# Rearranging the opening of a tuned Fourier-mixing and GEGLU kernel, and starting its first chunk's second layer sooner

## The chip, the cores and the metric

The kernel runs on one core of a Trainium2 chip. The metric is the device time of one execution in microseconds (us); lower is better. The profile's span (first to last instruction) is about 2 us shorter than the device time (632.1 and 633.91 us in the profiled run of the kernel before). Engines are named as in the profile: PE is TensorE (PEld its weight loads), DVE is VectorE, ACT is ScalarE, POOL is GpSimd, and SPq is the queue of DMA issues of SyncE. L695 is line 695 of the kernel that the profile belongs to, so the same statement has another number after the change.

## The reference

```python
# x: (8, 3008, 256); w_gate, w_val: (256, 1536); w_out: (1536, 256); all float32
X = np.fft.fft(x, axis=1)
X = np.fft.fft(X, axis=2)
y = X.real.reshape(24064, 256)
g = y @ w_gate
gelu = 0.5 * g * (1.0 + erf(g / sqrt(2)))
out = (gelu * (y @ w_val)) @ w_out
```

## The kernel before

Each of the 8 batches is folded (rows t and -t are added), transformed by matmuls into `EO`, and sent through the two layers in three chunks of 512 or 481 columns. A chunk has 12 *slots*, one for each 128 of the 1536 hidden features; there are 288 slots. A slot has five layer-1 matmuls on PE, two GELUs on ACT, three vector operations on DVE and one product on POOL. The layer-2 work of a chunk is 24 pieces of four matmuls, done two to a slot in the slots of the *next* chunk; the transform of the next batch fills gaps ("fill"), and POOL folds the batch after. Before slot 0 stands the opening: it builds the transform's constants, loads and folds batch 0, and makes the first weights.

The opening, with fillers (`warm`, dummy matmuls that keep PE busy):

```python
    def opening():
        # x of rows 9 to 16 and 0 loaded plainly by SyncE, then POOL's queue:
        pool_consts()
        pool_consts2()                      # holds the 1.35 us iota into par
        index_consts(0)
        cast_mirror(0, 9, 8)                # first gather of x
        cast_forward(0, 1, 8)
        cast_mirror(0, 5, 4)
        cast_mirror(0, 1, 4)
        index_consts(1)
        cast_mirror(0, 0, 1)
        for f0, n in ((0, 256), (256, 256), (512, 1024)):
            load_w(f0, n)
        for q in range(4):
            load_wo(q)
        # ...
        warm(11)
        vec_consts()
        g_phases()
        # ... more constants on DVE and ACT
        t_columns()
        t_phases()
        t_sin()
        warm(10)
        # ... gelu_table, t_write, identities, cw_rest, then:
        fold_piece(9, 4)
        stage1(2)
        warm(4)
        fold_piece(13, 4)
        fold_piece(5, 4)
        warm(2)
        stage1(1)
        warm(3)
        fold_piece(0, 1)
        stage1(3)
        warm(2)
        fold_piece(3, 2)
        fold_piece(1, 2)
        stage1(0)
        make_w(0, 0, 256, engine="V")()
        ch(0, 0)()
        ch(0, 1, "V")()
        make_w(1, 0, 256, engine="V")()
        tp_e(0, 0)()
        tp_o(0, 0, "V")()
```

The loads of batch 2 and the loop over the slots. `load_part` issues a plain load from SyncE and a gather from POOL (the mirrored rows):

```python
        for k, s in ((0, 18), (1, 19), (2, 19)):
            at(fill, s, lambda k=k: load_part(2, k))
        # ...
        for i, (parts, fc) in enumerate(blocks):
            if fc == 0 and i:
                assert not pend
                pend = list(works[i // NFC - 1])
            parts["G"][fc]()
            if i == 0:
                behind_first_gate()
            if before:
                before[0]["g"][before[1]]()
            parts["V"][fc]()
            if pend:
                pend.pop(0)()
            for f in pool.pop(i, []):
                f()
            if before:
                before[0]["v"][before[1]]()
            if pend:
                pend.pop(0)()
            for f in fill.pop(i, []):
                f()
            before = parts, fc
```

SyncE issues one after another: stores of a finished group of 128 tokens, and in every batch from the third on the write of the half-transformed batch to memory and its read in another layout (`z_read`):

```python
    def z_read(b):
        def run():
            st = state(b)
            st["Z"] = Z_tile()
            z = z_dram[b % 2]
            n = (NK // 2) * C
            nc.sync.dma_start(
                out=_sub(st["Z"], [[1, n]], 0), in_=ap_replace(z, ap=[[n, 128], [1, n]], offset=z.offset))
        return run
```

## Time and profile before

| before | us |
|---|---|
| median of the first 3 runs | 634.19 (633.90 to 634.34) |
| span of the profiled run | 632.1 |
| first layer-1 matmul (gate, E half; then O half) | 20.47; 21.11 |
| first GELU of slot 0, 12, 17, 25, 31, 287 | 21.52, 45.86, 59.22, 77.01, 91.32, 614.95 |

The slot times are starts of the first GELU of a slot (L638 in the timeline).

PE is nearly always busy (98%), so I looked for time where it is not: in the opening, in the first chunk and at stalls.

The chain of waits of the kernel before in the opening (start, length, what):

```profile
1.54 1.35 POOL par L281
3.42 0.56 POOL idx L268
...
4.26 5.73 DMA xb<-in_x_dram,idx
...
11.79 1.46 PE ps_o L757 x4
...
17.09 0.56 DVE A_sb L475
...
20.36 0.71 DVE EO_sb L556
```

A POOL fill, an index column and the gather's 5.73 us come first; then fillers (L757) at half clock (the clock record reads 0.50 from 11.9 us on for 3.4 us) stand in front of stage 1.

The timeline of the kernel before, with the first folds of batch 2 and the layer-2 matmul that waited behind them (the bracket is the idle time of the engine before the instruction, and what ended it):

```profile
20.47 0.38 PE L622 MATMUL ps_g<-EO_sb,W_sb 128*128 128x512 bf16 x1
21.11 0.38 PE L622 MATMUL ps_g<-EO_sb,W_sb 128*128 128x512 bf16 x1 [0.26 <-DVE EO_sb L556]
...
75.97 0.21 POOL L216 TENSOR_TENSOR ab_sb<-x_raw,x_raw 94x8 f32<-94x8 f32 x1 [1.80 <-DVE ve_sb L656]
...
80.92 0.28 PE L695 MATMUL ps_o<-Wo_sb,h_sb 128*128 128x256 bf16 x1 [0.32 <-POOL h_sb L671]
```

The windows view of the kernel before (busy time of PE, PEld, DVE, ACT, POOL; then the clock granted to TensorE, 1.00 being full speed, DMA share, GB/s):

```profile
80.00:85.00 5.00, 4.68 (x36) 2.90 (x34) 3.66 (x7) 3.60 (x9) 5.00 (x5) 1.00 0.32 81
```

### The profile page before, as it was taken

To read this page: it belongs to the slowest core of one execution; us is meant where nothing else is said; L and a number is where in the kernel's file an instruction comes from. 1 tells how busy PE (TensorE), PEld (TensorE's weight loads), DVE (VectorE), ACT (ScalarE), POOL (GpSimd) and SP (SyncE) were. 2 spreads that over 40 slices of the span, in tenths; PEclk is the share of its full clock that TensorE was granted. 3 is DMA by queue.
4 is the path that set the end of the run, shared out by engine and by line. 5 is a ranking of instruction groups with operands and counts; after the bars stand their busy time and mean duration, and the time that the engine had idled before them with its cause. 6 is when DMAs were issued, how large, how long until landed. Compare 5 with 4: busy or idle time off the path is not lost.

```text
span 632.1 us, 13032 instructions
## 1 busy us (share of the span) xinstructions
PE 618.9 (98%) x4285; PEld 407.4 (64%) x4285; DVE 580.9 (92%) x937; ACT 432.7 (68%) x855; POOL 505.7 (80%) x511
## 2 busy tenths in 40 slices
PE   7999999999999999999999999999999999999997
PEld 3446666666666666666666666666666666666666
DVE  7698889999899989999999999999999999999992
ACT  6787777666766667666776767766776766666651
POOL 8599799989997998879998799968988555555651
PEclk8999999999999999999999999999999999999999
DMA  8931925535454352633635325633222232221123
GB/s 152 179 61 26 250 63 147 139 99 138 121 146 107 91 140 65 167 84 100 156 93 155 93 66 138 153 92 104 57 53 57 75 104 54 52 51 38 43 51 80
DMA packets 51994, 63.84 MB, mean 101 GB/s; under 512 B 7783, under 2 KB 47194, under 8 KB 49530
## 3 DMA queue, kind: packets, MB, share of 16 engines
q1 hardware_dynamic: 45238, 47.23, 28.9%
q0 software_dynamic: 6096, 15.29, 11.5%
q8 instruction: 33, 0.54, 0.3%
q10 hardware_dynamic: 592, 0.49, 0.3%
q14 instruction: 35, 0.29, 0.1%
HBM read 38.86 MB, written 29.38 MB: 108 GB/s over the span
## 4 chain that ended last, share of the span: by engine, by line
PE 87%; DMA 4%; DVE 3%; POOL 2%; ACT 2%; issue 1%; POOLq 0%; DVEq 0%; ACTq 0%
PE ps_o L695 36%; PE ps_g L622 27%; PE ps_v L622 17%; DMA Z_sb<-z 3%; PE ps_dft L508 2%; PE ps_dft L544 2%; POOL h_sb L671 1%; DVE v_sb L669 1%; DMA xb<-in_x_dram,idx 1%; DVE h_sb L667 1%; PE ps_o L757 1%; PE ps_dft L574 1%; ACT gelu_sb L638 1%; DVE ve_sb L656 1%; PE ps_g L695 0%
## 5 line engine op out<-in xcount | busy, mean ns | idle before, releaser
L671 POOL TENSOR_TENSOR h_sb<-gelu_sb,v_sb 128x512 bf16<-128x512 bf16 (+1 forms) x288 | 328.7, 1144 | 106.3 <-DVE v_sb L669 92.0
L695 PE MATMUL ps_o<-Wo_sb,h_sb 128*128 128x256 bf16 (+1 forms) x2232 | 334.9, 273 | 1.0 <-POOL h_sb L671 1.0
L695 PEld LDWEIGHTS <-h_sb 128*128 128x128 bf16 (+1 forms) x2304 | 228.8, 100 | 112.5 <-POOL h_sb L671 2.7
L656 DVE SCALAR_TENSOR_TENSOR ve_sb<-EB_sb,yw,ps_v 128x512 f32<-128x512 bf16 (+1 forms) x288 | 212.1, 737 | 32.8 <-PE ps_v L622 29.0
L638 ACT ACTIVATE gelu_sb<-ps_g 128x512 bf16<-128x512 f32 (+1 forms) x288 | 169.6, 589 | 96.4 <-PE ps_g L622 93.0
L622 PE MATMUL ps_g<-EO_sb,W_sb 128*128 128x512 bf16 (+1 forms) x864 | 231.2, 375 | 2.7 <-ACT gelu_sb L647 2.0
L622 PE MATMUL ps_v<-EO_sb,W_sb 128*128 128x512 bf16 (+1 forms) x576 | 214.4, 375 | 0.5 <-ACT W_sb L423 0.5
L667 DVE TENSOR_TENSOR h_sb<-gelu_sb,ps_v 128x512 bf16<-128x512 bf16 (+1 forms) x288 | 195.0, 677 | 1.1 <-ACT gelu_sb L647 0.7
L669 DVE SCALAR_TENSOR_TENSOR v_sb<-ve_sb,ps_v 128x512 f32<-128x512 f32 (+1 forms) x288 | 192.6, 669 | 0.0
L622 PEld LDWEIGHTS <-W_sb 128*128 128x128 bf16 x1440 | 136.8, 98 | 82.3 <-issue 4.2
L647 ACT ACTIVATE gelu_sb<-ps_g 128x512 bf16<-128x512 f32 (+1 forms) x288 | 169.1, 587 | 0.0
L714 ACT ACTIVATE out_sb<-ps_o 128x512 f32<-128x512 f32 x92 | 54.9, 597 | 36.1 <-PE ps_o L695 36.0
L224 POOL TENSOR_TENSOR eo_sb<-ab_sb 94x512 bf16<-94x512 f32 (+1 forms) x60 | 66.6, 1110 | 0.1
L554 ACT ACTIVATE EO_sb<-ps_dft 128x512 bf16<-128x512 f32 (+1 forms) x44 | 26.0, 590 | 22.5 <-PE ps_dft L544 20.5
L511 ACT ACTIVATE S_sb<-ps_dft 96x512 bf16<-96x512 f32 x48 | 28.2, 587 | 11.3 <-PE ps_dft L508 11.3
L217 POOL TENSOR_TENSOR ab_sb<-x_raw,x_raw 94x508 f32<-94x508 f32 (+1 forms) x30 | 33.0, 1101 | 0.0
L220 POOL TENSOR_TENSOR ab_sb<-x_raw,x_raw 94x508 f32<-94x508 f32 (+1 forms) x30 | 32.9, 1096 | 0.0
L158 POOL DMA_INDIRECT x_raw<-in_x_dram,idx x18 | 17.0, 945 | 2.8 <-issue 0.6
L508 PE MATMUL ps_dft<-eo_sb,G 94*96 94x256 bf16 x102 | 19.2, 274 | 0.0
L544 PE MATMUL ps_dft<-TP,Z_sb 128*128 128x128 bf16 (+1 forms) x188 | 18.2, 218 | 0.5 <-DVE Z_sb L496 0.5
L544 PEld LDWEIGHTS <-Z_sb 128*128 128x128 bf16 x192 | 14.5, 98 | 2.4 <-DVE Z_sb L496 0.7
L757 PE MATMUL ps_o<-gelu_sb 128*128 128x512 bf16 x32 | 11.1, 498 | 1.2 <-DVE col L305 1.2
(128 smaller groups left out, 173.5 us busy)
## 6 DMA issues: line engine op xcount, KB each, us to landing
out_dram<-out_sb SPq DMA_DIRECT2D x361, 64.0 KB
x_raw<-in_x_dram SPq DMA_DIRECT2D x10, 768.0 KB
Z_sb<-z SPq DMA_DIRECT2D x6, 768.0 KB
z<-S_sb SPq DMA_DIRECT2D x6, 576.0 KB
EB_sb<-yrow SPq DMA_DIRECT2D x14, 128.0 KB
x_raw<-in_x_dram SPq DMA_DIRECT2D x2, 640.0 KB
z<-S_sb SPq DMA_DIRECT2D x6, 192.0 KB
EB_sb<-yrow SPq DMA_DIRECT2D x7, 120.2 KB
```

The costliest lines, as they stand in the source:

```text
L217: eng.tensor_tensor(ab(0, 1, up), fwd(1, up), mir(255, down), op=ALU.add)
L224: eng.tensor_tensor(_sub(eo, [[C, nj], [1, 128]], j0 * C + g * 128), ab(0, 0, [[1, 128]]), ab(1, 0, [[1, 128]]), op=op)
L544: nc.tensor.matmul(ps[:, o : o + n], st["Z"][:, pair, g * 128 : g * 128 + 128], _sub(TP, [[1, n]], g * 128), start=True, stop=True)
L622: nc.tensor.matmul(ps[:, :n], W[nm, part][:, fs], src, start=start, stop=stop, **kw)
L638: nc.scalar.activation(gl[:, 0, :n], pg[:, :n], AF.Gelu)
L647: nc.scalar.activation(_sub(gl, [[-1, n]], TOK + n - 1), pg[:, :n], AF.Gelu)
L656: nc.vector.scalar_tensor_tensor(ve[:, :n], EB_bufs[b][:, c0 : c0 + n], yw[:, fc : fc + 1], pv[:, :n], op0=ALU.mult, op1=ALU.add)
L667: nc.vector.tensor_tensor(st["h"][:, fc, 0, :n], gl[:, 0, :n], pv[:, :n], op=ALU.mult)
L669: nc.vector.scalar_tensor_tensor(_sub(vv, [[-1, n]], n - 1), ve[:, :n], 2.0, pv[:, :n], op0=ALU.mult, op1=ALU.subtract)
L671: nc.gpsimd.tensor_tensor(st["h"][:, fc, 1, :n], gl[:, 1, :n], vv[:, :n], op=ALU.mult)
L695: nc.tensor.matmul(pso[:m, half], st["h"][:, fc, sign, h0 : h0 + m], Wo_sb[:, fc, :], start=(fc == 0), stop=(fc == NFC - 1),)
L714: nc.scalar.activation(_sub(osb, [[1, 2 * C]], 0, part_num=m), pso[:m, :], AF.Copy)
```

## The change

The intent: issue the gather of x before the constants; compute fewer phases, and share the rest between engines; place fewer fillers (12 + 3 + 6 instead of 11 + 10 + 4 + 2 + 3 + 2); issue the second batch's x casts in one run ahead of slot 0; put POOL's folds of batch 1 out of slots 11 to 13; and do six of the first chunk's layer-2 pieces in slots 6 to 14.

```diff
@@ index: written as integers, no float column
-        nc.gpsimd.iota(col_i[:, i : i + 1], pattern=[[0, 1]], base=base, channel_multiplier=-1, **IOTA)
+        nc.gpsimd.memset(idx, 0)
+        nc.gpsimd.iota(idx[:NP, :], pattern=[[0, 1]], base=base, channel_multiplier=-1)
@@ opening, POOL's queue
         pool_consts()
-        pool_consts2()
         index_consts(0)
         cast_mirror(0, 9, 8)
+        pool_consts2()
+        cast_mirror(0, 5, 4)
         cast_forward(0, 1, 8)
-        cast_mirror(0, 5, 4)
-        cast_mirror(0, 1, 4)
         index_consts(1)
         cast_mirror(0, 0, 1)
-        for f0, n in ((0, 256), (256, 256), (512, 1024)):
+        cast_mirror(0, 1, 4)
+        for f0, n in ((0, 256), (256, 256), (512, 512), (1024, 512)):
             load_w(f0, n)
... (w_out in two loads instead of four)
+        xb[1] = xb_tile(1)
+        cast_forward(1, 9, 8)
+        cast_mirror(1, 9, 8)
+        cast_forward(1, 0, 9)
+        for j0, nj in ((5, 4), (1, 4), (0, 1)):
+            cast_mirror(1, j0, nj)
@@ opening, the rest (identities, CW and TP writes move from ACT to DVE,
@@ phases from DVE to ACT; helpers cut)
-        warm(11)
+        warm(12)
... (constants)
-        warm(10)
... 
+        warm(3)
+        fold_piece(9, 4)
+        t_reduced()
+        t_sin()
         gelu_table()
+        s1(0, 2, 0)()
+        s1(0, 2, 1)()
+        warm(6)
+        fold_piece(13, 4)
+        cw_rest()
         t_write()
-        stage1(2)
-        warm(4)
-        fold_piece(13, 4)
         fold_piece(5, 4)
-        warm(2)
... (warm(3) and warm(2) go too)
+        make_w(1, 0, 256)()
+        tp_e(0, 0, 0, "AV")()
+        tp_e(0, 0, 1, "AV")()
+        minus[0]()
@@ plan: x casts of batch 1 leave slots 0 to 5
-        slot_of = [6 + i * 13 // len(ops) for i in range(len(ops))]
+        slot_of = [6, 7, 8, 9, 10, 14, 15, 16, 17, 18]
@@ feed: layer 2 of the first chunk
+        first = works[0]
+        sooner = {6: [first[0]], 7: [first[3]], 10: [first[1]], 11: [first[4]], 13: [first[2]], 14: [first[5]]}
+        works[0] = first[6:]
...
+            two = sooner.pop(i, []) if i <= NFC + 2 else [pend.pop(0) for _ in range(2) if pend]
```

## The prediction

> **What bounds the kernel now.** Two regimes. From 53 us on it is TensorE: the windows view gives PE busy 148.7 to 149.9 us in each of three 150 us stretches, and the chain of waits is 87% PE. The change touches nothing there. The first 53 us differ.
> (a) Opening, to the first layer-1 matmul at 20.47 us (second half 21.11). The chain of waits: POOL fills `par` (an iota of 1.35 us), index column (0.56), issue (0.28), first gather of x (issued 4.26, landed 9.99), DVE folds, PE. PE idles from 9.12 to 10.84; the granted clock then reads 0.50 from 11.9 to 15.3, and filler and stage-1 matmuls at that clock are on the chain until 17.1, though DVE is free from 15.5.
> (b) First chunk, 20.5 to 45 us: no layer-2 work; a slot takes 1.85 to 2.0 us, set by DVE (0.74+0.60+0.60 on the chain) and ACT, with PE partly idle (4.10 of 5 us busy in 40 to 45).
> (c) Slots 12 to 14, 44.9 to 53.4 us: 8.6 us for about 7.0 us of PE work; the chain goes through DVE and a POOL product (1.16 at 51.56). POOL is busy all the time: folds of the second batch, 2.5 us a pair, and earlier six DMA issues of 0.6 to 1.0 us in slots 0 to 5 delay it.
>
> **What the change does.**
> 1. Gather first: `par`, row constants and the float index column leave the POOL prefix. Issue moves from 4.26 to about 1.9, landing from 10.0 to about 7.8. It now overlaps the plain loads (1.75 to 5.75), so I count 2.2, not 2.4 us. DVE must be free: the folded phases trade a 0.72 and parts of a 0.58 and a 1.00 us operation for smaller ones, but copies, identities and TP writes move from ACT to DVE. I get DVE ready at 7.9: a tie.
> 2. Fillers placed between stage-1 pieces. [...] The clock should stay at 1.0. DVE then sets the pace, its last stage-1 copy ending at 16.1 instead of 17.65. Evictions split over ACT and DVE save about 0.3 us each; deferring the `M` copy removes a 0.5 us wait. First gate at 18.4: gain 2.1 us.
> 3. Four layer-2 pieces (4 x 0.44 us) move into slots 6, 7, 10, 11, where PE has about 0.4 us of slack; two stay in 13 and 14. Slots 12 to 14 then hold 5.2 us of PE work and become bound by DVE, about 6.5 to 6.9 us: gain 1.7.
> 4. Second x cast issued before slot 0 (POOL idles 7.3 us there), pool folds moved out of slots 11 to 13: makes 3 possible; alone perhaps 0.2.
>
> Sum: 2.1 + 1.7 + 0.2 = 4.0 us, all on the critical path since PE is saturated afterwards. Predicted 630.2 us, 80% range 628.4 to 631.9. Faster by over 2% (12.7 us) 0.5%, within 2% 99%, slower 0.5%.
>
> **What would show it.** Gather landing near 7.8; first fold near 8; no 0.50 stretch of clock; first gate near 18.4; chunk 0 still about 24.5 us long; slots 12 to 14 near 6.9 us with no wait on POOL; PE unchanged from 55 us on.
>
> **What would make it wrong.** Gather and plain loads slowing each other (landing after 9); DVE, with more work, stretching the opening; added pieces lengthening chunk 0; later second-batch folds (slots 14 to 18) delaying its stage 1 or the folds of batch 2, where POOL is waited for at 77 to 81 us; weights landing late.

"The clock should stay at 1.0" is my expectation alone, and the 2.1 us of the opening rested on it in part. (In point 1 the 2.4 us are 4.26 less 1.9; the step down to 2.2 is an estimate of mine.)

## More of the kernel before

The page of the kernel before. The first lines give busy time, share of the span and number of instructions of an engine; the q8 line is one of the DMA queues (packets, MB, share of 16 engines); the last is the chain of waits that ended last, by engine:

```profile
span 632.1 us, 13032 instructions
...
PE 618.9 (98%) x4285; PEld 407.4 (64%) x4285; DVE 580.9 (92%) x937; ACT 432.7 (68%) x855; POOL 505.7 (80%) x511
...
q8 instruction: 33, 0.54, 0.3%
...
PE 87%; DMA 4%; DVE 3%; POOL 2%; ACT 2%; issue 1%; POOLq 0%; DVEq 0%; ACTq 0%
```

The queue line is easily read past: 33 packets of together 0.54 MB are 16 KB each. They are instruction fetches, as the page calls their kind.

The timeline of SyncE's queue of the kernel before: the three plain loads of batch 2, and four stores ahead of the z read of a later batch:

```profile
63.78 1.32 SPq L152 DMA_DIRECT2D x_raw<-in_x_dram  x3
...
356.43 2.40 SPq L616 DMA_DIRECT2D out_dram<-out_sb  x4
358.93 0.52 SPq L530 DMA_DIRECT2D Z_sb<-z  x1
```

And the chain of waits of the kernel before at that place: PE has to wait for z to land, so the moment of its issue counts.

```profile
358.93 4.82 DMA Z_sb<-z
...
363.79 0.22 PE ps_dft L574
```

## The result, and the profile after

The change made the kernel slower: 638.36 us (636.77 to 638.68, 4 runs) against 634.05 us of before (633.82 to 634.34, 4 runs). The ratio is 1.0063, 95% interval 1.0045 to 1.0081; by the 2% limit that is "the same", but the sign is sure. A ratio here and below is the mean time of one kernel's fast runs over that of the other's fast runs of the same rounds, so it is not quite the ratio of the medians quoted.

The predicted gain of 4.0 us was in fact a loss of 4.3. The spans of the two profiles differ by 4.8 us, and the slots show where:

| stretch (first GELU to first GELU) | before | after | difference |
|---|---|---|---|
| start to slot 0 | 21.52 | 21.38 | -0.14 |
| slot 0 to 12 | 24.34 | 24.85 | +0.51 |
| slot 12 to 17 | 13.36 | 11.72 | -1.64 |
| slot 17 to 25 | 17.79 | 17.75 | -0.04 |
| slot 25 to 31 | 14.31 | 17.93 | +3.62 |
| slot 31 to 287 | 523.63 | 526.14 | +2.51 |

Up to slot 25 the changed kernel is 1.31 us ahead. Everything is lost later, in parts of the program that the change did not touch. In the last stretch the loss sits in one slot of each of four batches: the steps that end at the first GELU of slots 127, 163, 199 and 235, 36 apart, took 2.65, 3.38, 3.26 and 2.98 us, before 2.33, 2.49, 2.22 and 2.37. That is 2.86 us; other steps give 0.35 back.

The page of the changed kernel:

```profile
span 636.9 us, 12960 instructions
...
PE 615.4 (97%) x4225; PEld 407.7 (64%) x4274; DVE 580.2 (91%) x944; ACT 433.1 (68%) x852; POOL 503.7 (79%) x508
...
q8 instruction: 33, 0.54, 0.4%
...
PE 85%; DVE 4%; POOL 3%; DMA 3%; ACT 2%; issue 2%; SPq 0%; POOLq 0%; DVEq 0%; ACTq 0%
```

Weight loads are counted in full: 4274 instead of 4285, because the change has 21 fillers where there were 32. (The matmul count differs more, but some matmul records are missing: on both pages 2232 stand against 2304 weight loads in layer 2.) In the compiled programs PE's list has 8531 rows instead of 8553: 22 instructions fewer. Most of the loss turns out to hang on this small number.

The chain of waits of the changed kernel in the opening:

```profile
6.99 1.25 PE ps_v L387 x10
...
9.44 0.67 ACT small_t L393 x2
10.14 0.24 DVE small_t L260
...
12.52 0.56 DVE TP L404
...
15.93 0.87 PE ps_dft L437 x4
16.82 0.60 ACT W_sb L443
```

The gather has left the chain, as intended. In its place stand the constants themselves: five tiny matmuls, ACT's phases, DVE's reduction and writes.

The timeline of the changed kernel: the first fold, DVE's wait for ACT's phases, stage 1, the first gate, the first folds of batch 2 and the layer-2 matmul behind them.

```profile
7.87 0.19 DVE L216 TENSOR_TENSOR eo_sb<-x_stage,xb 94x8 bf16<-94x8 f32 x1 [0.56 <-DMA xb<-in_x_dram,idx]
...
10.14 0.23 DVE L260 TENSOR_SCALAR small_t<-small_t 128x128 f32<-128x128 f32 x1 [0.91 <-ACT small_t L393]
...
13.65 0.50 PE L493 MATMUL ps_dft<-G,eo_sb 94*128 94x96 bf16 x4 [2.72 <-DVE eo_sb L217]
...
20.07 0.38 PE L651 MATMUL ps_g<-EO_sb,W_sb 128*128 128x512 bf16 x1
...
20.97 0.38 PE L651 MATMUL ps_g<-EO_sb,W_sb 128*128 128x512 bf16 x1 [0.53 <-DVE EO_sb L585]
...
76.61 0.22 POOL L216 TENSOR_TENSOR ab_sb<-x_raw,x_raw 94x8 f32<-94x8 f32 x1 [4.41 <-DMA x_raw<-in_x_dram,idx]
...
81.56 0.28 PE L725 MATMUL ps_o<-Wo_sb,h_sb 128*128 128x256 bf16 x1 [2.05 <-POOL h_sb L700]
```

POOL waits 4.41 us for the gather of batch 2 with that fold at the head of its queue, the products behind it come late, and PE idles 2.05 us for one of them. The windows view of the changed kernel shows what follows:

```profile
80.00:85.00 5.00, 3.44 (x14) 1.95 (x15) 1.22 (x2) 2.23 (x4) 5.00 (x6) 0.68 0.13 33
```

PE is busy for 3.44 of 5 us and the granted clock averages 0.68: the clock record reads 0.50 for 3.4 us from 81.8.

The timeline of SyncE's queue of the changed kernel: the stores ahead of batch 2's plain loads, and those ahead of the same z read as above.

```profile
59.87 3.52 SPq L645 DMA_DIRECT2D out_dram<-out_sb  x4
63.66 1.32 SPq L152 DMA_DIRECT2D x_raw<-in_x_dram  x3
...
358.72 3.31 SPq L645 DMA_DIRECT2D out_dram<-out_sb  x4
362.13 0.52 SPq L556 DMA_DIRECT2D Z_sb<-z  x1
```

```profile
362.13 4.80 DMA Z_sb<-z
...
366.97 0.22 PE ps_dft L603
```

The last fence is the chain of waits. The z read takes as long as before, 4.8 us, but the four stores ahead of it took 3.31 instead of 2.40 us to issue. Of the four, the third alone is slow: 1.49 us where it was 0.59. I looked for what else happened at that moment, and found the 16 KB packets of q8. For the z reads of batches 3 to 7, from the records of single issues and packets (us from the span's start):

```text
z read issued   third store: start, length   nearest q8 packet: start, length
before
   209.90          208.56  0.59                206.27  0.94
   284.88          283.55  0.59                280.76  1.10
   358.93          357.60  0.59                354.74  1.25
   433.16          431.80  0.59                428.98  1.22
   507.13          505.79  0.59                503.08  1.14
after
   212.77          210.86  1.16                210.70  0.95
   287.35          285.48  1.12                285.29  0.93
   362.13          359.89  1.49                359.89  1.12
   437.31          434.99  1.58                434.96  1.22
   511.93          509.87  1.31                509.85  0.95
```

In the changed kernel the fetch begins within 0.2 us of the third store, in each of these; before, it fell about 2.3 to 2.9 us ahead of it, while SyncE was waiting. (At the z read of batch 2 the nearest fetch was 5.8 us away before and 7.0 after, and no store was slow.) Over the whole trace 27 of 33 fetches stand beside an issue of over 0.8 us, before 4 of 33; the issues of over 0.8 us number 31 and 7. (Three more fetches overlapped an issue that stayed short, before five more: a fetch beside an issue does not always go with a long one.)

On PE itself these fetches hardly show: in the kernel before it was busy without a break from 1 us before to 1 us after 29 of the 33, and beside the other four it idled 0.26 us at most. But in the changed kernel the 27 SyncE issues beside a fetch took 0.83 to 1.83 us, where a store otherwise takes 0.59 (median).

Why would that repeat in each batch? The two traces give the spacing. Between one packet of q8 and the next lie 256 PE instructions in the median, in both (the weight loads in between, doubled for their matmuls; single spacings are 200 to 304, the mean is 254.5 before and 254.6 after). So I read the packets as PE's instructions, one fetch for about 256 of them: PE's list of 8531 rows would need 33.3, and 33 were seen; and a_plus11, below, moves them by PE instructions alone. A group of stores comes every three slots; three slots have 3 x 13 matmuls with as many weight loads, 78 instructions, and some fills, by estimate about 85 (the doubled weight loads of slots 31 to 287 give 84.4 in the kernel before), a third of 256. So fetches and groups of stores run nearly in step, one fetch to three groups, and the phase between them, once set in the opening, lasts. And each fetch keeps its place in the count of PE instructions: the doubled weight loads ahead of it differ by 5 between the two traces on average (-18 to 48). Taking 22 instructions out of the opening thus puts every later fetch about 22 instructions later in the program.

### The profile page after: what moved, and what is told of

Read it like the earlier page. It is cut to its first block, busy times and chain, and to the rows that moved or that the text cites. A ratio compares the mean times of both kernels' runs of the same rounds, so it can differ in the third digit from the quotient of the medians.

```text
span 636.9 us, 12960 instructions
## 1 busy us (share of the span) xinstructions
PE 615.4 (97%) x4225; PEld 407.7 (64%) x4274; DVE 580.2 (91%) x944; ACT 433.1 (68%) x852; POOL 503.7 (79%) x508
## 4 chain that ended last, share of the span: by engine, by line
PE 85%; DVE 4%; POOL 3%; DMA 3%; ACT 2%; issue 2%; SPq 0%; POOLq 0%; DVEq 0%; ACTq 0%
PE ps_o L725 34%; PE ps_g L651 26%; PE ps_v L651 17%; DMA Z_sb<-z 3%; POOL h_sb L700 3%; PE ps_dft L534 2%; PE ps_dft L570 2%; DVE v_sb L698 1%; PE ps_dft L437 1%; ACT gelu_sb L667 1%; PE ps_dft L515 1%; ACT W_sb L443 1%; PE ps_dft L603 1%; DVE ve_sb L685 0%; PE ps_g L725 0%
## 5 line engine op out<-in xcount | busy, mean ns | idle before, releaser
L583 ACT ACTIVATE EO_sb<-ps_dft 128x512 bf16<-128x512 f32 (+2 forms) x45 | 26.3, 586 | 24.0 <-PE ps_dft L570 21.6
L607 ACT ACTIVATE yrow_sb<-ps_dft 4x128 bf16<-4x128 f32 x21 | 5.4, 257 | 9.4 <-PE ps_dft L603 9.4
```

## The experiments

Theory P (phase): the 22 missing PE instructions put PE's instruction fetches onto SyncE's stores, one issue in a group is held up, and what stands behind it in SyncE's queue (the z reads, the plain loads of batch 2) comes late. Rival M: addresses, reordered loads and more traffic made DMAs slower. "Slow issues" are SyncE issues over 0.8 us, "hits" fetches beside one; both are counted in the profiled run. Kernels whose names begin with a_ start from the changed kernel, those with b_ from the one before.

| run | PE rows | median us (lowest to highest) | ratio to before, 95% | hits | slot 0 | slots 25 to 31 | slots 31 to 287 |
|---|---|---|---|---|---|---|---|
| before | 8553 | 634.05 | 1 | 4 | 21.52 | 14.31 | 523.63 |
| the change | 8531 | 638.36 | 1.0063 (1.0045 to 1.0081) | 27 | 21.38 | 17.93 | 526.14 |
| a_plus11 | 8553 | 633.53 (633.18 to 634.37) | 0.9996 (0.9979 to 1.0012) | 4 | 22.14 | 15.30 | 523.68 |
| b_less11 | 8531 | 639.34 (638.07 to 639.73) | 1.0087 (1.0067 to 1.0106) | 27 | 21.86 | 15.25 | 527.39 |
| a_late11 | 8553 | 634.86 (634.78 to 635.40) | 1.0018 (1.0001 to 1.0035) | 6 | 20.74 | 17.86 | 523.55 |
| a_warm17 | 8553 | 633.41 (631.61 to 635.12) | 0.9999 (0.9969 to 1.0028) | 4 | 21.57 | 14.57 | 523.41 |
| a_fwd | 8531 | 634.48 (633.79 to 635.27) | 1.0010 (0.9995 to 1.0026) | 24 | 21.64 | 14.03 | 526.39 |
| a_plus43 | 8617 | 633.87 (632.82 to 634.05) | 0.9999 (0.9984 to 1.0015) | 22 of 34 | 22.27 | 14.83 | 523.49 |
| a_nosooner | 8553 | 634.68 (633.69 to 636.01) | 1.0022 (1.0004 to 1.0040) | 4 | 22.82 | 14.66 | 523.17 |
| best1 | 8553 | 632.51 (630.44 to 633.09) | 0.9982 (0.9968 to 0.9995) | 4 | 19.98 | 14.03 | 522.92 |
| best2 | 8553 | 633.51 (631.69 to 634.87) | 0.9995 (0.9980 to 1.0010) | 4 | 20.58 | 14.03 | 522.91 |
| c_order | 8553 | 632.78 (631.70 to 633.02) | 0.9973 (0.9958 to 0.9988) | 4 | 22.31 | 14.03 | 523.38 |
| c_gather | 8553 | 632.02 (630.50 to 633.39) | 0.9974 (0.9958 to 0.9989) | 4 | 19.84 | 14.03 | 523.37 |
| b_fwd | 8553 | 639.81 (639.53 to 640.47) | 1.0093 (1.0077 to 1.0108) | 6 | 21.79 | 13.81 | 522.80 |

All were correct. The runs of before beside them had medians of 633.67 (first four), 633.30 (next four) and 634.16 (last four).

**a_plus11: give the changed kernel its 22 instructions back.** One-column matmuls in a gap in which PE idles:

```diff
         warm(6)
+        tiny(11)   # matmul(ps[:, 0:1], idle[:, 0:128], idle[:, 0:1])
```

> The changed kernel plus 11 one-column dummy matmuls (22 TensorE instructions) in the 2.7 us in which PE idles at 10.9 us, so that it has as many PE instructions as the kernel before (8553, not 8531). Theory P (phase): the 16 KB instruction fetches, one per 256 PE instructions, fall in the SyncE queue's bursts of stores because 22 PE instructions went away, and hold one DMA issue for 1.0 to 1.8 us each. With the count restored: at most 12 of the 33 fetches beside a slow issue (27 now), z waits of slots 127, 163, 199, 235 back to about 0.2 us each (2.9 us gained), the second stage of loads earlier, total about 632.5 to 634. Rival theory M (memory and bandwidth: other tile addresses, reordered loads, more in flight make DMAs slower): count of slow issues and time stay, 637 to 639.

Measured: 633.53 us, 4.8 less than the changed kernel by the medians, though nothing but 11 useless matmuls was added, and its profiled opening was even 0.76 us longer. The hits fall from 27 to 4. The timeline of SyncE's queue of a_plus11, at the same z read:

```profile
357.29 2.40 SPq L645 DMA_DIRECT2D out_dram<-out_sb  x4
359.80 0.52 SPq L556 DMA_DIRECT2D Z_sb<-z  x1
```

The stores issue in 2.40 us again. Theory P holds; M, which knows no reason for this, falls.

**b_less11: take 22 instructions from the kernel before.** The last four groups of fillers of the opening go:

```diff
-        warm(4)
...
-        warm(2)
...
-        warm(3)
...
-        warm(2)
```

> The kernel before without its last 11 filler matmuls in the opening (4, 2, 3 and 2), so 8531 PE instructions as in the changed kernel; nothing else differs. Theory P: slow DMA issues beside the fetches appear (over 20 of 33) and the slots after 60 lose about 2.5 us, whatever the opening gains or loses (0 to 1 us): 635 to 637.5. Theory M: no such stalls, 633 to 634.5.

Measured: 639.34 us, as slow as the changed kernel, 27 hits, and 3.76 us lost from slot 31 to 287 (I had expected 2.5). The timeline of SyncE's queue of b_less11:

```profile
358.51 3.72 SPq L616 DMA_DIRECT2D out_dram<-out_sb  x4
362.34 0.52 SPq L530 DMA_DIRECT2D Z_sb<-z  x1
```

The loss can be made in the old kernel without any part of the change except its instruction count. (Its opening, without these fillers, came to slot 0 0.34 us later than in the profile of before, at a clock of 0.50 for 6.8 us.)

**a_late11: the same 11 matmuls, but in slot 34.** Behind the stall of slots 26 to 30, in front of the z reads:

```diff
+        def late():
+            ps = psum("dft")
+            for _ in range(11):
+                nc.tensor.matmul(ps[:, 0:1], II[:, 0, 0, :], TP[:, 0, 0, 0:1], start=True, stop=True)
+
+        at(fill, 34, late)
```

> The changed kernel with the same 11 dummy matmuls put in slot 34 (about 98 us), behind the long stall of slots 26 to 30. Theory P: fetches after 100 us no longer meet the bursts, the z waits go (2.5 us gained, less about 0.5 for the dummies), the stall of slots 26 to 30 stays at about 3.6 us: 636 to 637. Theory M: 638.5 to 639.

Measured: slots 25 to 31 still take 17.86 us, slots 31 to 287 fall to 523.55. So the two losses are separate, and the second hangs on the phase alone, not on anything set up in the opening. The total of 634.86 is better than I wrote: the profiled run reached slot 0 0.64 us earlier than that of the changed kernel, with the same opening.

**a_warm17: full fillers instead of tiny ones in the gap.**

```diff
-        warm(6)
+        warm(17)
```

> The changed kernel with 17 instead of 6 full filler matmuls behind the first stage-1 piece: same PE instruction count as before, and PE busy through the gap of 10.9 to 13.65 us. Theory P as in a_plus11; in addition the granted clock should stay at 1.0 from 13 to 16.6 us, and the first gate come 0.3 to 0.8 us earlier than 20.07: 631.5 to 633.5. Theory M: 637 to 638.5, only the opening's part gained.

Measured: 633.41 us, 4 hits: the phase part as expected. The clock part failed: it still fell to 0.50 for 3.4 us, only sooner, from 9.5 us on. And the first gate came at 20.25, 0.18 later than in the change instead of 0.3 to 0.8 earlier: at that clock the 17 fillers kept PE until 14.8, and stage 1 behind them began at 14.88 (13.65 in the change). In the profiled runs with the changed kernel's opening the half-clock stretch began at 13.5, 9.8 and 8.3 us (the change, a_late11, a_fwd), in a_fwd once more at 15.1. What sets that start is not shown. One profile of an opening therefore is a draw: in these three runs slot 0 came at 21.38, 20.74 and 21.64 (a_fwd issues the loads of batch 2 in it).

**a_fwd: the bad phase kept, the plain loads of batch 2 early.**

```diff
-        for k, s in ((0, 18), (1, 19), (2, 19)):
-            at(fill, s, lambda k=k: load_part(2, k))
+        pieces2 = ((9, 8), (1, 8), (0, 1))
+        for piece in pieces2:
+            at(fill, 10, lambda piece=piece: load_forward(2, *piece))
+        for piece, s in zip(pieces2, (18, 19, 19)):
+            at(fill, s, lambda piece=piece: load_mirror(2, *piece))
```

> The changed kernel (8531 PE instructions, so in the bad phase) with the three plain loads of batch 2 issued in slot 10 instead of 18 and 19; the gathers stay. Theory P with its second part (slots 26 to 30 stall because the plain loads and gathers of batch 2 share the DMA engines from 65 us on, and the slow issue at 61.3 us pushed the plain loads back): the first gather lands by about 70 us instead of 76.6, slots 25 to 31 take about 14 us instead of 17.9, the z waits remain: 634.5 to 635.5. Rival (the stall comes from VectorE or GpSimd being late with the later folds, or from the halved clock alone): 637.5 to 639.

Measured: 634.48 us; slots 25 to 31 take 14.03 us, and the z waits stay (526.39). The timeline of POOL and the windows view of a_fwd:

```profile
72.42 0.22 POOL L216 TENSOR_TENSOR ab_sb<-x_raw,x_raw 94x8 f32<-94x8 f32 x1
```

```profile
80.00:85.00 5.00, 5.00 (x37) 3.18 (x36) 4.38 (x8) 3.61 (x8) 4.10 (x5) 1.00 0.25 63
```

The fold no longer waits, PE stays busy and the clock at 1.00. So the stall of slots 26 to 30 is a deadline set by the loads of batch 2, which begin at about 65 us in both kernels: by estimate some 3.3 MB (17 rows of 94 KB, loaded plainly and gathered), or 13 us at the 249 KB a us that the queues moved from 65 to 80 us in the kernel before. Seven runs, ordered by how late the first fold starts against slot 25; the other seven fit (a_nosooner -0.69 and 14.66, a_plus43 -0.52 and 14.83, the five with early loads -2.9 to -3.5 and 13.81 to 14.03):

| run | first fold of batch 2 | slot 25 | fold after slot 25 by | slots 25 to 31 |
|---|---|---|---|---|
| a_fwd | 72.42 | 75.95 | -3.53 | 14.03 |
| before | 75.97 | 77.01 | -1.04 | 14.31 |
| a_warm17 | 75.11 | 75.88 | -0.77 | 14.57 |
| b_less11 | 77.27 | 77.37 | -0.10 | 15.25 |
| a_plus11 | 76.40 | 76.45 | -0.05 | 15.30 |
| a_late11 | 75.89 | 75.05 | +0.84 | 17.86 |
| the change | 76.61 | 75.70 | +0.91 | 17.93 |

Both the lead of the earlier slots and the start of the loads enter. In the two runs past +0.8 the clock also reads 0.50 for 3.4 us, from 81.8 and 81.5. In the changed kernel the phase did most of it: a slow store of 1.73 us just before the loads kept them at 63.66, though the kernel was 1.3 us ahead. In a_warm17, with the phase restored and slot 25 at nearly the same time (75.88 against 75.70), they go out at 62.70, and slots 25 to 31 take 3.36 us less.

**a_plus43: the phase moved by a whole group of stores.**

```diff
         warm(6)
+        tiny(43)
```

> The changed kernel with 43 dummy one-column matmuls where a_plus11 had 11: 86 PE instructions more than the changed kernel. Three slots, one group of stores, are about 85 PE instructions (78 for the layers, the rest fills), so theory P says that the fetches meet the bursts again: over 18 of 33 fetches beside a slow issue, z waits and the stall of slots 26 to 30 as in the changed kernel, plus up to 2 us of opening for the dummies: 637.5 to 641. If it were not the phase but simply more PE instructions or a longer opening that helps: 633 to 636, under 12 slow issues.

Measured: the hits come back, 22 of 34, as expected, but not the time: 633.87 us. My expectation was wrong in its last step. The timeline of SyncE's queue of a_plus43 at the z read:

```profile
356.71 2.40 SPq L645 DMA_DIRECT2D out_dram<-out_sb  x4
359.22 0.52 SPq L556 DMA_DIRECT2D Z_sb<-z  x1
```

Here the fetch comes 7.3 us ahead of the third store: it hits another group of the three, behind which nothing urgent stands. By themselves the slow stores cost nothing here (523.49 us from slot 31 to 287 with 22 hits, 523.41 in a_warm17 with 4); in the changed kernel, where the z reads stand behind them in the queue, it was 526.14. This also speaks against "more PE instructions are slower", since it has the most.

**a_nosooner: a_warm17 without the layer-2 pieces brought forward.**

```diff
-        sooner = {6: [first[0]], 7: [first[3]], 10: [first[1]], 11: [first[4]], 13: [first[2]], 14: [first[5]]}
-        works[0] = first[6:]
+        sooner = {}
...
-            two = sooner.pop(i, []) if i <= NFC + 2 else [pend.pop(0) for _ in range(2) if pend]
+            two = [pend.pop(0) for _ in range(2) if pend]
```

> a_warm17 (good phase) without the six layer-2 pieces brought forward; all else as there. If the pieces are worth what the slots of the profile say (0.8 us lost in slots 5 to 11, 2.0 gained in 12 to 15): slots 0 to 17 take 1.0 to 1.3 us longer than in a_warm17 and the time is 634.2 to 634.8. If the gain there comes from the moved folds and casts alone: no difference, 633.2 to 633.7.

Measured: slots 0 to 12 take 24.47 us and 12 to 17 take 12.39; in a_warm17 24.85 and 11.72. The pieces therefore gain 0.67 us late and lose 0.38 early: 0.29 us net, not 1.0 to 1.3. Against before (24.34 and 13.36) the rest of the gain, 0.84 us, is there without them. The folds and casts moved on POOL are the likely cause; they were not tested alone, and other edits (the pieces in which the weights are loaded) differ too. The total of 634.68 agrees with the expectation only because this run's opening was 1.25 us longer (clock at 0.50 for 6.8 us); the slots, not the total, answer the question.

**best1: a version made to beat both.** The good phase, early plain loads, and DVE's order in the opening:

```diff
+ the loads of a_fwd; warm(13), warm(3), warm(16)
         fold_piece(9, 4)
-        t_reduced()
-        t_sin()
-        gelu_table()
         s1(0, 2, 0)()
         s1(0, 2, 1)()
         fold_piece(13, 4)
-        cw_rest()
-        t_write()
+        t_reduced()
+        t_sin()
+        gelu_table()
         fold_piece(5, 4)
... (cw_rest ahead of fold_piece(1, 4), t_write last)
```

> A version made to beat both: the changed kernel with 32 full fillers (13, 3, 16; 8553 PE instructions), the plain loads of batch 2 in slot 10, and VectorE's fold of rows 13 to 16 ahead of its wait for ScalarE, TP and CW writes behind the folds. Theory P: good phase (under 12 slow issues), slots 25 to 31 about 14 us, first gate 0.5 to 1.3 us earlier: 631 to 632.5. If the opening is paced by something else than VectorE's order and the clock: 632.5 to 633.5.

Measured: 632.51 us, ratio 0.9982 to before, the interval below 1: by the medians it is 0.8 us below the kernel before (633.30 in the same rounds) and 5.9 below the changed kernel (638.36, measured earlier). c_order and c_gather, which are next, are below the kernel before by at least as much (0.9973 and 0.9974). best1's profile shows slot 0 at 19.98 with the clock at 1.0 from 7.2 us on.

**best2, c_order, c_gather: what in the opening paces it.** best2 puts the weight product and its eviction behind the two products for the first gate; c_order puts the change's order back into best1; c_gather puts the constants back ahead of the first gather.

```diff
 # best2
-        make_w(1, 0, 256)()
         tp_e(0, 0, 0, "AV")()
         tp_e(0, 0, 1, "AV")()
-        minus[0]()
+        make_w(1, 0, 256, engine="V")()     # M copy moved behind the first gate's extras
 # c_gather
-        cast_mirror(0, 9, 8)
         pool_consts2()
+        cast_mirror(0, 9, 8)
```

> best1 with the second weight product of the opening and its eviction behind the two products that feed the first gate, that eviction on VectorE, and the M copy behind the first gate's extras. In best1's trace ScalarE's 0.60 us weight eviction at 17.28 stands ahead of its half of the E eviction, and the second product waits for its PSUM buffer behind it. If that order holds the first gate back: first gate at about 17.8 and its second half at 18.5 instead of 18.66 and 19.56, slot 0 at 19.0 to 19.5 instead of 19.98, total 631.3 to 632.2. If PE or Z paces it: no change from best1 (632.5).

> best1 with the changed kernel's order of VectorE's and ScalarE's opening work put back (t_reduced ahead of the fold of rows 13 to 16; TP and CW writes ahead of the fold of rows 5 to 8); fillers 13, 3, 16 as in best1. If VectorE's 0.91 us wait for ScalarE's phases and the writes ahead of the fold pace the opening: slot 0 0.8 to 1.3 us later than best1 at the same clock, total 633 to 634. If the clock alone made best1's opening faster: slot 0 near 20.0, total 632.5.

> best1 with the row constants put back ahead of the first gather (about 0.85 us later issue). If the landing of the first gather paces the opening: slot 0 later by 0.7 to 0.9 us. If VectorE, ready at about 7.3, gives slack only later (its order of work paces): under 0.4 us. Total 632.5 to 633.5.

best2 missed: 633.51 us. The timeline of best2 shows the first gate later, not earlier (18.66 in best1):

```profile
19.51 0.60 PE L437 MATMUL ps_dft<-w_raw,CW 128*128 128x256 bf16 x4 [0.94 <-DVE EO_sb L585]
...
20.16 0.38 PE L651 MATMUL ps_g<-EO_sb,W_sb 128*128 128x512 bf16 x1
```

The weight product now waits 0.94 us for an eviction, and the gate stands behind it in PE's queue. c_order's profile reached slot 0 at 22.31, but at half clock for 3.4 us, and its time, 632.78, is not told from best1's; it is inconclusive. c_gather reached slot 0 at 19.84, no later than best1, and took 632.02. But it did not test what it was made for. Its gather was issued 0.53 us later (2.43 against 1.90; I had reckoned with 0.85), and yet the first fold that needs it began at 8.09, in best1 at 8.22. So issuing this gather half a microsecond sooner did not land it sooner; whether a later landing would pace this opening is not shown. In both runs the chain of waits goes through ACT's phases there and not through the gather.

**b_fwd: the early plain loads in the kernel before.** The same edit as a_fwd.

> The kernel before, with only the three plain loads of batch 2 issued in slot 10. If plain loads and gathers of batch 2 share the DMA engines and so hold GpSimd in both kernels: slots 25 to 31 take 14.0 us or less instead of 14.3, the first fold is not later than 73 us instead of 75.97, and the time falls by 0.3 to 1.0 us, 632.5 to 633.3. If the stall exists in the changed kernel alone: no change.

Slots 25 to 31 did shorten, to 13.81 us, so the deadline was there before the change too. But the time rose to 639.81 us. "Slot 10" is no time for SyncE: its queue was empty, so it issued the loads at 16 us, as soon as their buffer was free, while the weights were on their way. The timeline of PE of b_fwd:

```profile
29.66 1.04 PE L417 MATMUL ps_dft<-w_raw,CW 128*128 128x512 bf16 x2 [4.82 <-DMA w_raw<-in_moe_w_val_dram]
```

From 21 to 25 us each of the two queues moved about 28 packets a us, the plain loads in packets of some 7 KB, the weights in packets of 2 KB: 200 and 56 KB a us. In the kernel before, without the plain loads, the queue of the weights moved 186 to 198. So at equal numbers of packets the queue with the smaller ones got 56 KB a us of about 256; why the numbers were equal is not shown. In a_fwd and best1 the loads go out early too, but slots 1 to 4 hardly stall (slots 0 to 12 take 24.85 and 25.13 us there, 24.85 in the change); I did not find out why (their weights are issued 0.9 to 2.4 us sooner and in smaller pieces).

## Why the prediction was wrong

The step that failed is the sum's last clause: "all on the critical path since PE is saturated afterwards", with "The change touches nothing there". Being ahead at slot 17 did not carry to the end, and the change did touch the rest, through the position of PE's instruction fetches. In the two profiles the sum was off by 8.8 us (4.0 forecast as gain, 4.8 lost): 6.1 in slots 25 to 287, 2.0 in the opening, 0.8 in slots 0 to 17.

1. *Gather first* (predicted landing 7.8). Right: the first fold that needs it started at 7.87. But it was off the critical path then: the changed kernel's chain of waits goes through the constants and ACT's phases instead. (c_gather was to test this, but its landing did not move.)
2. *Opening, gain 2.1 us.* Mis-sized: the first gate came at 20.07, not 18.4, and slot 0 came 0.14 us earlier in the profile of the change, 0.78 earlier to 0.12 later in two other runs with the same opening. "The clock should stay at 1.0" was wrong: PE idled 2.72 us before 13.65, for DVE, which had itself waited 0.91 us for ACT's phases; the clock then read 0.50 for 3.4 us. What the traces show is that PE's longest idle time ahead of the half-clock stretch was 2.72 us here and 1.72 us in the kernel before. The eviction of the second weights on ACT stands ahead of the first gate; I had not put it in the chain. How much is order and how much is the clock stays open.
3. *Slots 12 to 14, gain 1.7 us; chunk 0 unchanged.* Slots 12 to 17 gained 1.64, but slots 0 to 12 lost 0.51: net 1.13. The attribution was wrong: the layer-2 pieces are worth 0.29 net, and 0.84 came without them, probably from POOL's moved folds and casts, which I had put at 0.2.
4. *What I listed as a danger, "the folds of batch 2, where POOL is waited for at 77 to 81 us", is where 3.62 us went*, but not because the folds were later: their data has a deadline of its own, set by DMA, as a_fwd shows. Coming sooner cost little by itself: a_warm17 reaches slot 25 1.13 us ahead of the kernel before and takes 0.26 us longer for slots 25 to 31. The rest is the phase, which held the loads back.
5. *Not foreseen at all:* the phase of the instruction fetches, 2.51 us from slot 31 on, and most of item 4, where restoring it brings 17.93 us down to 15.30 (a_plus11) and 14.57 (a_warm17). a_plus11, b_less11 and a_late11 show it in both directions.

With the phase restored the change is worth what is left of its gains: a_warm17 gives 0.9999 (0.9969 to 1.0028), that is, nothing that three rounds can show (the span of its profile is 1.1 us shorter). How a fetch of PE would hold an issue of SyncE inside the chip is not shown here; that they coincide (27 of 33 fetches in the changed kernel), and that moving the one frees the other (4 of 33 in a_plus11), is.

## What to carry to other kernels

When a change removes or adds instructions and the time moves in places it does not touch, compare the lengths of single DMA issues in the two traces, and look at what the instruction queue does at the same moment; a few dummy instructions tell a phase effect from a real one (here 11 dummy matmuls took the hits from 27 to 4 and the time from 638.36 to 633.53 us). Time won ahead of a load whose start or rate does not move can be lost at that load (here 1.31 us ahead at slot 25, then 3.62 us lost by slot 31): find the next deadline before adding the gain to the total. And the slot of a statement is not the time of its issue: in b_fwd SyncE's empty queue issued the loads of slot 10 at 15.74 us, ahead of slot 0, as soon as their buffer was free.
